# Another order for the later operations of a fused attention and mixer kernel

## The chip, the cores and the metric

The kernel runs on one core of one Trainium2 chip. The metric is device time in microseconds for the whole program, one launch, lower being better. The engines are named as in the profile: PE is TensorE, DVE is VectorE, ACT is ScalarE, POOL is GpSimd and SP is SyncE. Each engine takes its own instructions in the order in which the program wrote them, and waits for others by semaphores.

## What is computed

Eight batches of causal attention in blocks (8 heads, 576 positions, head size 64) are followed by a mixer: two products along the positions ("token") and two along the channels, each pair with a relu between, each with its input added.

```python
def _attn_ref(q, k, v):                      # q, k, v: 8 x 8 x 576 x 64
    scores = scale * np.matmul(q, k.transpose(0, 1, 3, 2))
    mask = block_i >= block_j                # blocks of 64 positions
    scores = np.where(mask, scores, -1000000000.0)
    attn = np.exp(scores - np.max(scores, axis=-1, keepdims=True))
    attn = attn / (np.sum(attn, axis=-1, keepdims=True) + 1e-09)
    return np.matmul(attn, v)

def _moe_ref(x, w_tok1, w_tok2, w_ch1, w_ch2):   # x: 8 x 576 x 512
    h = np.maximum(x.transpose(0, 2, 1) @ w_tok1, 0.0) @ w_tok2
    u = x + h.transpose(0, 2, 1)
    return u + np.maximum(u @ w_ch1, 0.0) @ w_ch2
```

Inputs and output are float32; the matrix products work on bfloat16 copies.

## The kernel before

The kernel first lists all its work as some 1,590 numbered operations, each a closure that emits one or a few instructions, with the operations it depends on. It then emits them in one written order, the text `ORDER`. A word of that text is an operation's number, a letter for its engine (T is PE, A is ACT, D is DVE, P is POOL, S is SP) and, for an operation that opens PSUM banks, a letter for each bank: a to d are the tiles `mm`, e to h the tiles `late`, s and t the two pairs `sc` of the start. So `644Tadgb` is score set 644 on PE in the banks a, d, g and b.

```python
for word in ORDER.split():
    digits = word.rstrip("abcdefghstADPST")
    o, letters = self.ops[int(digits)], word[len(digits):]
    o.engine = self.ENGINE[letters[0]]
    assert all(d.n in done for d in o.deps)
    for letter, (pools, note) in zip(letters[1:], o.take):
        note["pool"], note["slot"], note["home"] = pool_of[letter], self.SLOTS[letter][1], letter
```

The order of the words of one letter is thus the order of that engine's queue; the words decide as well which of two possible engines does an evacuation of PSUM (ACT or DVE), a tail (DVE or POOL) or a late output (SP or ACT). Words of different engines stand in one text because the framework derives the semaphores from the order of emission: an operation emitted later waits for one emitted earlier where they touch the same tile.

The operations of a batch, with the lines under which the profile shows them:

- Loads of q and k (L413, POOL, one DMA each) and their transposition on DVE in halves (L437). For batch 4, 759 loads k and 762 loads q of the first four heads; 760 and 761 transpose k, 763 and 764 transpose q. For batch 3 the second four heads have the transpositions 602, 603 (k) and 605, 606 (q).
- Loads of v (L463, POOL, five DMAs): 607 to 611 for batch 3, 771 to 775 for batch 4, 938 to 942 for batch 5.
- Scores (L562, PE): three sets for each half of the heads, each in four banks, and for each bank an exponential on ACT (L768; L581 in batch 0). For batch 3 the sets are 612, 619, 624 and 644, 651, 656; those of batch 4 begin at 776, of batch 5 at 943, of batch 6 at 1038, of batch 7 at 1136. The first score set of batch 0 is in two parts, 174 and 175, with the exponentials 176 and 177.
- Tails, a small copy and a clearing of part of the exponentials (L590 and L595, POOL or DVE), such as 617 and 618, or 980 and 981.
- Heads: products with v (L612, L665, PE), a reciprocal (L632, L687, DVE) and a scaling (L638, L693, DVE).
- Token products (L803, L807, then L898, L929, PE), relus (L789 on ACT, L791 on DVE) and u additions (L913, DVE), such as 681 and 685, and from batch 2 on a transposition by DMA (L965, L975, SP).
- The first channel product in seven products a group instead of eight (L1099, and L1226 for two batches at once, PE), with sums held back as a copy (`keep`, L395 on ACT or L397 on DVE, such as 547), a copy that seeds two further banks (`seed`, the same lines), joins (L1138 and L1259, DVE, such as 554), relus (L789, L791) and clips (L1151 and L1272 on ACT, L1153 and L1274 on DVE, such as 542). Where a seeded bank was not filled in full before, one opening matmul of 512 columns is put ahead (`cover`).
- The second channel product likewise (L1360, PE), with sums (L1342, DVE) and folds into the output (L1406, DVE), and the outputs (L1451, L1435, SP or ACT).

PE works at the attention of one batch between the channel products of earlier ones: the operations of batch 3's attention stand among those of batch 1's first channel product (526 to 574), batch 4's among batch 2's (690 to 738), batch 5's among batch 3's (857 to 905).

Of the kernel before, what the change touches and what calls it, by code (L numbers as in the profile page):

```python
# [27 lines left out]
class Plan:  # L28
# [73 lines left out]
    23D 25D 21D 31D 7D 174Tst 176A 175T 177A 81Ta 76Tb 195A 197D 196A 33D 198D 60Tc 61Td 201Ts 180Tt 202A 80Ta 35P 182Ts  # L102
# [11 lines left out]
    331D 332D 441A 432D 431D 358T 359A 450Tgceh 427P 429D 322D 323D 428D 369Td 370T 169P 453A 452A 363Tf 364T 335D 454A
    371D 451A 365A 482Tbeac 393D 484A 504Th 336D 470Tgfde 483A 485A 486A 474A 502Tb 472A 503A 471A 445Tacef 447A 505D
    514Th 168P 167P 170D 171D 172D 173D 611P 510Tb 506Tg 598P 599D 511D 394D 448A 446A 515A 508Tc 433P 512Te 513D 509D
    507D 395D 396D 524Ta 473A 397Thd 403Tb 449A 525A 434P 406D 398A 399T 443P 444P 402D 437P 477Tfaec 480A 407T 522Tg
    479A 523A 410D 595P 597D 596D 518Te 519A 411T 412D 436P 435P 455Ta 458Th 461Tg 608P 604P 600D 601P 464Te 475P 476P
    481A 456D 465D 466D 478A 496Tc 462D 516Tf 517A 463D 457D 459D 460D 520Tb 521A 413T 414D 605D 499Te 497D 609P 467Tf
    468D 500D 498D 501D 612Tgbah 616A 613A 615A 614A 469D 415T 545Tgh 526D 493Tc 530Tae 531Tf 527D 494D 533A 487Tb 495D  # L120
# [8 lines left out]
    779A 820Tedgb 585T 824A 821A 823A 577D 690D 781P 782P 694Taf 695Tb 935P 691D 578D 942P 799Te 696D 842Tg 697A 692D
    698Tb 699A 587T 702T 693D 843A 848Tg 586D 800D 801D 700T 849D 589T 588D 703D 701A 822A 590D 808Tegac 930D 932P 931D  # L130
    846Td 793Tb 591T 809A 810A 811A 794D 795D 847D 592D 796Te 797D 798D 812A 938P 813P 814P 815Tgabc 818A 816A 805Td
    806D 928D 941P 704T 705D 724Tbh 819A 802Te 803D 804D 844Tg 807D 845D 706D 725Tc 940P 727A 730T 817A 850Te 851D 726A
    709Tad 854S 937D 712A 828Tc 829D 728Tg 830D 710Te 707T 715T 729A 716A 734T 711A 927D 732T 731D 855S 708D 713Ta
# [10 lines left out]
    1079A 1080A 1081A 594S 1124D 1017Tc 1018D 755T 1123D 1121D 1083A 1015Tb 1034P 756D 1016D 1078A 1037P 1070Tdeca 757S
    1067Tg 1064Th 1068D 1065D 1066D 1073A 1074A 1128P 1058Tf 1059D 1072A 1069D 873D 1125P 1060D 1071A 1130D 1104Tc 1105A
    1133P 1132P 1061Tb 1013Ta 1055Th 1143Tegdf 1014D 1145A 1146A 1056D 1057D 1129D 1062D 1063D 1075P 1076P 1090Tc 1144A
    1091D 1092D 1127D 1102Ta 1103A 1147A 1093Th 1094D 1095D 1136Tgdbe 1137A 1114Tc 1139A 1140A 1126D 1099Ta 1100D 1101D
    1108Tf 1109D 1110Tg 1096Th 1097D 1138A 1141D 1098D 1087Tb 1088D 1115A 1175Teadf 1112Tc 1089D 1011Th 1012D 1019S
    1113D 1179A 1336Tb 1177A 1176A 1178A 1168Tfaeh 1337A 1172A 906D 1171A 1111D 1170A 1106Td 1107D 1116S 910Tbc 907D
    1148Thgea 1149A 1152A 911D 1151A 914Td 1142P 916T 908D 1169A 1180Thaef 1182A 909D 912T 1183A 1173D 1184A 917D 915D  # L150
    1134P 918T 913D 1181A 1174D 1131P 1135P 1162Ta 1163D 1164D 1153Te 1154D 1155D 1191Tf 1192D 1193D 1159Th 1197Tb 1198D
    1160D 1150A 1161D 1117S 1165Tg 1166D 1167D 920T 921D 1199D 1194Ta 1020S 1156Te 1157D 1158D 1185Tf 1334Th 1335A 1186D
    1187D 1188Tg 1189D 1190D 1195D 1196D 922T 1234Thb 923D 856S 1348Te 1237A 1349A 1200D 1249Tcf 1240T 1252A 1241A 919D
    1118S 1201D 1202D 1250Tg 1251D 1235Ta 1236A 1253Td 1254D 1238Te 1279Tah 1255T 1256A 1259T 1239D 1242T 1257T 1203D
    1282A 1243D 1350Tg 1283Tc 1260D 1258D 1285T 1351A 1262T 1263D 1286D 1284A 1204Tde 1280Tg 1244T 1281D 1205Tf 1207A
    1208Ta 1206A 1210T 1360Tg 1209A 1214T 1211A 1361A 924S 1245D 1215D 1264Tdf 1267A 1247T 1212T 1289T 1213D 1290D 1248A
    1287T 1288D 1344Tg 1345D 1217T 1218A 1265Tb 1270T 1219Tac 1266A 1271D 1268Te 1269D 1356Tg 1357D 1222A 1220Tb 1292T
    1293A 1358Td 1359D 1364S 1221D 1223Tg 1274T 1275D 1338Th 1225T 1479D 1224A 1229T 1354Td 1339D 1230D 1355D 1277T
    1278A 1226A 1227T 1228D 1272T 1273D 1232T 1233A 1294D 1295D 1261D 758S 1291A 1342Tb 1343D 1216A 1347S 1352Th 1498Taf
    1298Tcd 1501A 1353D 1362S 1296D 1363S 1297D 1276D 1302Tg 1480D 1481D 1299A 1304T 1305D 1504T 1231A 1483Tbe 1484Th  # L160
    1485A 1300T 1486A 1308T 925S 1246A 1301D 1482D 1303D 1309D 1489T 1314D 1502Tc 1503A 1306T 1307D 1340Th 1341D 1310T
    1505D 1490A 1315D 1487Tg 1488A 1508T 1499Th 1513Tab 1500A 1493T 1311D 1494D 1506T 1514Th 1516A 1517Td 1491T 1519T
    1520A 1509D 1518D 1492D 1515A 1346S 1496T 1523T 1507D 1510D 1521T 1524D 1316D 1511T 1512A 1497D 1414Tag 1312S 1417D
    1318Tch 1319D 1526T 1322Tf 1320T 1317D 1527A 1399Tbe 1402A 1522D 1365D 1415Td 1416A 1324T 1366D 1323D 1325D 1321D
# [1396 lines left out]
```

## Time and profile before

| | |
|---|---|
| three timed runs | 286.66, 287.95, 288.83 us; median 287.95 |
| the profiled execution | 285.7 us, its span in the profile 283.9 us |
| PE, DVE, ACT, POOL busy | 273.1, 247.0, 176.2, 73.7 us |
| granted PE clock | 1.0 throughout |
| moved by DMA | 31.94 MB in 64889 packets |

Times in the profile are microseconds from the start of the span unless marked ns. A row of the timeline gives the start, the length, the engine, the line of the source, the operation and its tiles, a count, and in brackets the idle time of the engine before it with what ended it. A row of the groups gives the count, the busy time, the mean ns of one, and the idle time before them. A row of the stretches gives the length of the stretch and, for each engine, its busy microseconds. Matmuls are pipelined and their shown lengths overlap, so the step between starts is the time that one takes.

### The profile page before, as it was taken

The numbers are of one execution on the slowest core, as the hardware profiler recorded it, in microseconds if no ns is written. First come the engines' busy times: TensorE is split into PE (matmuls) and PEld (weight loads), VectorE is DVE, ScalarE is ACT, GpSimd is POOL, SyncE is SP. The second block draws the span as 40 slices with busy tenths as digits, with TensorE's granted clock in tenths as the row PEclk, the third lists the DMA queues.
The fourth block names the chain that finished last, engine by engine and source line by source line (L and its number), as shares of the span: only waits on it lengthen the run. The fifth ranks groups of instructions, "written<-read, shape, count | busy, mean of one in ns | idle before, by whom it ended". The sixth has DMA issues, their size and how long they took to land.

```text
span 283.9 us, 9275 instructions
## 1 busy us (share of the span) xinstructions
PE 273.1 (96%) x3930; PEld 202.4 (71%) x3956; DVE 247.0 (87%) x525; ACT 176.2 (62%) x322; POOL 73.7 (26%) x125
## 2 busy tenths in 40 slices
PE   6798999999989999999999999999999999999995
PEld 2376574589667788886877668766688976468884
DVE  4578889999789989999999987887899998799994
ACT  3796969955978857799978875256464324634000
POOL 8986626701732054024351030000000000000000
PEclk9999999999999999999999999999999999999999
DMA  7999999992999456949499079012045301400165
GB/s 167 152 156 206 178 213 210 176 118 44 182 190 111 76 77 54 212 97 140 36 161 158 3 64 172 3 74 86 8 46 147 108 0 74 151 0 3 74 180 192
DMA packets 64889, 31.94 MB, mean 113 GB/s; under 512 B 53200, under 2 KB 55888, under 8 KB 64848
## 3 DMA queue, kind: packets, MB, share of 16 engines
q0 software_dynamic: 44896, 17.49, 52.9%
q1 hardware_dynamic: 19232, 12.82, 17.7%
q10 hardware_dynamic: 720, 1.05, 1.0%
q8 instruction: 31, 0.51, 0.7%
q14 instruction: 10, 0.08, 0.1%
HBM read 35.85 MB, written 9.44 MB: 159 GB/s over the span
## 4 chain that ended last, share of the span: by engine, by line
PE 83%; POOL 6%; DMA 5%; ACT 2%; issue 1%; DVE 1%; POOLq 0%
PE mm L1360 16%; PE late L1360 14%; PE late L1226 8%; PE late L1099 7%; PE mm L1226 5%; PE mm L1099 4%; PE late L562 4%; PE mm L562 3%; PE late L612 3%; PE mm L612 3%; DMA w_sb<-in_moe_w_tok_dram 3%; DMA qk_sb<-in_k_dram 3%; POOL vals L463 2%; ACT e_sb L768 2%; PE late L898 2%; PE mm L803 2%
## 5 line engine op out<-in xcount | busy, mean ns | idle before, releaser
L768 ACT ACTIVATE e_sb<-late 128x512 bf16<-128x512 f32 x83 | 48.3, 618 | 11.9 <-PE late L562 6.7
L768 ACT ACTIVATE e_sb<-mm 128x512 bf16<-128x512 f32 x85 | 49.0, 614 | 8.5 <-PE late L562 3.9
L437 DVE STREAM_TRANSPOSE qk_sb<-qk_sb 128x288 int32<-128x288 int32 (+1 forms) x65 | 42.4, 696 | 3.3 <-DMA qk_sb<-in_k_dram 2.2
L463 POOL DMA_DIRECT2D vals<-in_v_dram x45 | 37.3, 850 | 13.0 <-PE late L665 6.1
L1360 PEld LDWEIGHTS <-gT 128*128 128x128 bf16 x336 | 32.0, 98 | 6.0 <-issue 0.4
L1360 PEld LDWEIGHTS <-sums 128*128 128x128 bf16 x324 | 31.2, 98 | 5.3 <-issue 1.5
L562 PEld LDWEIGHTS <-qk_sb 32*64 32x64 bf16 (+1 forms) x1152 | 19.5, 103 | 17.1 <-issue 12.4
L562 PE MATMUL late<-qk_sb 32*64 32x64 bf16 (+7 forms) x494 | 27.9, 279 | 0.9 <-DVE gT L1138 0.7
L562 PE MATMUL mm<-qk_sb 32*64 32x64 bf16 (+7 forms) x514 | 27.6, 280 | 0.3 <-DVE qk_sb L437 0.2
L612 PEld LDWEIGHTS <-e_sb 128*128 128x128 bf16 x640 | 23.7, 97 | 4.1 <-issue 1.4
L1099 PEld LDWEIGHTS <-ws_sb 128*128 128x128 bf16 x192 | 18.2, 98 | 3.4 <-issue 0.9
L395 ACT COPY mm<-late 128x512 f32<-128x512 f32 x24 | 14.1, 592 | 10.3 <-PE late L1226 4.1
L590 POOL COPY vals<-e_sb 128x256 bf16<-128x256 bf16 x10 | 5.1, 506 | 51.6 <-ACT e_sb L768 51.6
L1226 PEld LDWEIGHTS <-ws_sb 128*128 128x128 bf16 x120 | 11.7, 98 | 8.1 <-issue 0.4
L789 ACT ACTIVATE gT<-late 128x512 bf16<-128x512 f32 x20 | 12.2, 619 | 8.0 <-PE late L1226 4.7
L612 PE MATMUL mm<-vals,e_sb 128*128 128x65 bf16 x370 | 15.8, 193 | 0.5 <-DMA vals<-in_v_dram 0.4
L638 DVE TENSOR_TENSOR x_sb<-mm,rinv 128x256 bf16<-128x256 f32 x37 | 15.4, 420 | 0.9
L1099 PEld LDWEIGHTS <-wc_sb 128*128 128x128 bf16 x144 | 15.1, 114 | 1.4 <-issue 0.4
L1226 PEld LDWEIGHTS <-wc_sb 128*128 128x128 bf16 x90 | 10.1, 113 | 5.7
L1360 PE MATMUL mm<-wd_sb,sums 128*128 128x256 bf16 x114 | 13.9, 273 | 0.0
L1226 PE MATMUL late<-e_sb,ws_sb 128*128 128x512 bf16 (+1 forms) x54 | 13.5, 356 | 0.0
L581 ACT ACTIVATE e_sb<-sc 128x1024 bf16<-128x1024 f32 (+2 forms) x14 | 11.6, 908 | 2.2 <-PE sc L562 2.2
(205 smaller groups left out, 653.3 us busy)
## 6 DMA issues: line engine op xcount, KB each, us to landing
out_dram<-o_sb SPq DMA_DIRECT2D x18, 256.0 KB, 2.4
qk_sb<-in_q_dram POOLq DMA_DIRECT2D x14, 288.0 KB, 6.4
qk_sb<-in_k_dram POOLq DMA_DIRECT2D x14, 288.0 KB, 6.3
vals<-in_v_dram POOLq DMA_DIRECT2D x28, 128.0 KB, 6.5
out_dram<-o_sb SPq DMA_DIRECT2D x7, 512.0 KB, 3.2
wc_sb<-in_moe_w_ch_dram POOLq DMA_DIRECT2D x8, 192.0 KB, 6.9
wc_sb<-in_moe_w_ch_dram POOLq DMA_DIRECT2D x3, 512.0 KB, 11.7
vals<-in_v_dram POOLq DMA_DIRECT2D x15, 64.0 KB, 5.3
```

The costliest lines, as they stand in the source:

```text
L395: nc.scalar.copy(dst, src)
L437: nc.vector.transpose(dst[:, 0:S, :] .rearrange("p s e -> p (s e)") .bitcast(I32) .rearrange("p (a k) -> p k a", k=NB)[:, k0:k1], raw2.bit ...
L463: nc.gpsimd.dma_start(out=t[128 - p : 128, J, hs, 0:64], in_=src)
L562: nc.tensor.matmul(out=home(n)[lo : lo + rows, c : c + w], lhsT=bar[r, 0] if j is None else kT[i][r, 64 * j : 64 * j + rows, par], rhs=bar ...
L581: nc.scalar.activation(dst, sc[SC.index(note["pool"])][:, :, cols], EXP, scale=scale)
L612: nc.tensor.matmul(out=u[:, I, 0:65], lhsT=e[:, h, c : c + 128], rhs=vt[:, J, head, 0:65], start=(J == 0), stop=(J == I),)
L638: nc.vector.tensor_tensor(out=xt[:, 0:4, 64 * head : 64 * head + 64], in0=u[:, :, 0:64], in1=ri[:, 0:4].to_broadcast([128, 4, 64]), op=MULT,)
L768: nc.scalar.activation(dst, bank_of(x), EXP, scale=scale)
L789: nc.scalar.activation(dst, src, RELU)
L1099: nc.tensor.matmul(out=bank_of(bank)[:, 256 * o_ : 256 * o_ + 256], lhsT=x(o_, m), rhs=y[:, :, m, :], start=opens, stop=m == 1, skip_group ...
L1226: nc.tensor.matmul(out=bank_of(bank)[:, 128 * c : 128 * (c + step)], lhsT=x(m), rhs=y[:, c : c + step, m, :], start=opens, stop=m == 1, sk ...
L1360: nc.tensor.matmul(out=bank_of(bank)[:, 256 * i : 256 * i + 256], lhsT=x[:, kk, 128 * i : 128 * i + 128], rhs=y[:, kk], start=first and i ...
```

## The change

Only the text `ORDER` changes. Word by word, the numbers are the same; what changes is their order, the bank letters and, for 73 operations, the engine. First, 175 moves ahead of 176:

```diff
-    23D 25D 21D 31D 7D 174Tst 176A 175T 177A 81Ta 76Tb 195A 197D 196A 33D 198D 60Tc 61Td 201Ts 180Tt 202A 80Ta 35P 182Ts
+    23D 25D 21D 31D 7D 174Tst 175T 176A 177A 81Ta 76Tb 195A 197D 196A 33D 198D 60Tc 61Td 201Ts 180Tt 202A 80Ta 35P 182Ts
```

From there to batch 3's attention only bank letters differ. From then on the order is another one. The part around the scores of batch 3:

```diff
-    490Tc 532A 418D 488D 491D 489D 492D 548A 536T 537A 534Td 535A 551T 602D 552A 624Tfbca 628A 625A 626A 528D 538T 539D
-    549Tg 550D 529D 540T 541D 627A 678Ta 679A 762P 617P 618P 619Tfdbc 622A 543T 544A 607P 620A 623A 546Ta 606D 759P 764D
-    761D 547A 676Tb 773P 621A 603D 760D 677A 553T 560Tce 774P 554D 555T 775P 563A 561Tf 763D 644Tadgb 562A 648A 566T
-    556D 646A 645A 684Tf 557D 567D 420S 685D 564Tb 647A 610P 558T 559A 565D 680Td 651Tcafg 655A 542D 652A 654A 653A 768P
...
+    490Tf 532A 418D 488D 491D 489D 492D 548A 536T 537A 534Te 535A 551T 602D 762P 617P 618P 607P 759P 773P 420S 419S 610P
+    528D 624Thgfb 552A 538T 606D 628A 540T 529D 627A 539D 678Ta 626A 603D 625A 549Tb 679A 619Tfegh 541D 550A 546Ta 622A
+    760D 553T 623A 763D 543T 620A 547D 676Tg 621A 761D 544A 644Thfae 542D 926P 677A 554D 555T 647A 764D 560Tbc 648A 556D
+    561Tg 929P 563A 680Ta 557D 765P 562A 684Te 681D 645A 566T 558T 685D 646A 564Ta 567A 649D 559D 651Tghfe 650P 565A
...
```

The part around the second half of batch 5's scores, where 1008 and 1010 change their engine:

```diff
-    892Te 991A 893D 593S 895Ta 1027P 890A 896A 1030P 1007Tb 1008A 740D 955Tdgef 959A 901T 741D 958A 956A 1009Tb 1022D
-    957A 989A 899T 960Tf 902D 904T 1010A 975Tedgc 972Tb 905A 900D 1026D 961D 962D 1035P 966Ta 967D 978A 976A 977A 743Thf
...
+    887D 1034P 990A 895Tf 988A 875D 889T 991A 1007Th 740D 989A 896A 890D 955Tdegb 741D 892Tc 959A 899T 1026D 956A 901T 893D
+    958A 1009Tb 957A 1008D 902D 975Tdgce 1010D 972Th 978A 904T 900D 979A 960Tb 1025D 969Tc 905A 743Tef 961D 976A 973D
...
```

And the end, with the last outputs:

```diff
-    1584T 1585D 1589A 1562T 1563D 1568S 1566T 1567D 1569A 1586T 1587D 1590A
+    1577D 1585D 1566T 1589A 1583D 1556T 1588A 1567D 1562T 1569S 1557D 1586T 1563D 1568S 1587D 1590S
```

On PE one instruction pair is added: product 1249 (L1226) gets one opening matmul.

More of the change, by code (lines that the diff above doesn't have):

```diff
@@ L114 @@
[L114 to L118, printed above, removed]
@@ L129 @@
[L129 to L133, printed above, removed]
@@ L144 @@
[L144 to L163, printed above, removed]
@@ new lines @@
+    1282A 1350Tb 1256A 1281A 1234Tcg 1351A 1344Td 1237A 1283Tb 1345D 1285T 1284A 1240T 1286A 1338Te 1241A 1250Td 1339D
+    1253Th 1251A 1287T 1202D 1254A 1348Tc 1288D 1203D 1259T 1349A 1257T 1238Tb 1258D 1289T 1239A 1235Te 1290D 1342Td
+    1236A 1244T 1291D 1343D 1356Tc 1242T 1245D 1219Tdh 1243D 1360Te 1260D 1220Tb 1361A 1357D 1262T 1222A 1292T 1364S
+    1263D 1221A 1340Te 1247T 1293D 1223Tb 1341D 1358Tc 1224A 1246D 1204Taf 1359D 1248A 1205Te 1225T 1207D 1206A 1264Tcg
+    1226A 1229T 1479D 1267A 1265Te 1230D 1208Td 1266A 1227T 1480D 1209D 1270T 1268Te 1271A 1214T 1269D 1212T 1354Tc
@@ new lines @@
+    1215D 1274T 1228D 1232T 1275D 1217T 1272T 1481D 1218A 1210T 1482D 1233A 1273D 1277T 1211A 1483Tbf 1278D 1347S 1484Th
+    1352Te 1294D 1485A 1298Tag 1295D 1363S 1302Th 1296D 1299A 1486A 1353D 1304T 1355D 1297D 1362S 1300T 1231D 1305D
+    1487Tc 1301D 1346S 1308T 1303D 1498Tae 1309D 1306T 1501A 1213D 1488A 1276D 1310T 1307D 1504T 1311D 1491T 1505A 1489T
+    1261D 1313S 1493T 1312S 1490A 1513Tad 925S 1502Tb 1516A 1499Th 1503D 1514Tg 1500A 1519T 1492D 1508T 1494D 1520A
+    1506T 1509D 1517Ta 1515A 1496T 1216D 1518A 1314D 1511T 1414Tch 1512A 1507D 1521T 1523T 1522D 1510A 1318Tbg 1524D
@@ new lines @@
+    1417A 1365D 1526T 1366D 1420T 1415Te 1315D 1421A 1322Ta 1416A 1527D 1319A 1497D 1418Tc 1316D 1320T 1419A 1367D
+    1429Tde 1321D 1324T 1432A 1317D 1323D 1424T 1435T 1425D 1422T 1436A 1433Tb 1368D 1326T 1423D 1434A 1325D 1430Tf
+    1327D 1439T 1431A 1427T 1332S 1399Tad 1428A 1328T 1402D 1440D 1437T 1405T 1438D 1442T 1406A 1384Tcf 1441D 1443A
+    1329D 1385Th 1387A 1403Ta 1400Tb 1386A 1330T 1404A 1401A 1409T 1331D 1407T 1390T 1333S 1408D 1369Tbe 1391A 1444Tgh
+    1410D 1372A 1388Ta 1412T 1389A 1375T 1413D 1447A 1373Tc 1394T 1525D 1374A 1376D 1370Td 1450T 1395D 1371A 1448Tb
@@ new lines @@
+    1426D 1392T 1449A 1445Td 1393D 1451A 1379T 1446A 1454T 1495D 1380D 1452T 1396A 1377T 1455D 1382T 1397T 1457T 1398A
+    1532Tag 1458D 1383A 1459D 1463Tdf 1460D 1467Te 1461D 1464A 1462D 1469T 1533D 1528D 1465T 1468D 1536Th 1466D 1453D
+    1471T 1529D 1456A 1470D 1538T 1530D 1378D 1473T 1472D 1381A 1411D 1477S 1534T 1531D 1474D 1574Tbd 1570D 1554Tce
+    1535D 1575A 1571D 1475T 1555A 1550D 1537D 1576T 1539D 1540T 1476D 1551D 1478S 1580T 1552D 1542T 1541D 1547S 1578Ta
+    1546S 1543D 1560T 1572D 1544T 1573D 1581D 1553D 1558Tf 1561D 1545D 1564T 1579D 1548S 1549A 1559D 1584T 1565D 1582T
```

67 lines of the change are left out of this document (39 added, 28 removed).

## The prediction

> **What bounds the kernel now.** I read the page first, then the busy time by stretches, then the waits of TensorE, and then the order of time around the one long wait.
>
> ```profile
> span 283.9 us, 9275 instructions
> PE 273.1 (96%) x3930; PEld 202.4 (71%) x3956; DVE 247.0 (87%) x525; ACT 176.2 (62%) x322; POOL 73.7 (26%) x125
> PEclk9999999999999999999999999999999999999999
> ```
>
> TensorE is busy 96% of the span, at the full granted clock in all slices. VectorE stands at 87%, so it is the second bound. Both must be seen by stretch:
>
> ```profile
> core 0: us, PE busy (x) PEld busy (x) DVE busy (x) ACT busy (x) POOL busy (x), PEclk, DMA share, GB/s
> 72.00:88.00 16.00, 14.94 (x225) 10.21 (x226) 13.23 (x26) 13.90 (x28) 8.24 (x13) 1.00 1.40 178
> 106.00:120.00 14.00, 13.89 (x280) 11.87 (x280) 13.82 (x31) 10.14 (x20) 3.30 (x5) 1.00 1.00 123
> 120.00:132.00 12.00, 12.00 (x170) 10.08 (x167) 11.26 (x26) 11.35 (x22) 4.62 (x8) 1.00 0.68 116
> 132.00:146.00 14.00, 13.95 (x309) 10.51 (x309) 12.92 (x30) 12.70 (x26) 4.79 (x8) 1.00 0.80 100
> 146.00:163.00 17.00, 16.79 (x375) 12.31 (x377) 16.40 (x44) 14.26 (x29) 3.03 (x5) 1.00 0.75 99
> ...
> 184.00:210.00 26.00, 25.84 (x179) 17.78 (x180) 21.97 (x36) 16.13 (x28) 0.00 (x0) 1.00 0.14 46
> 210.00:240.00 30.00, 29.95 (x249) 24.79 (x249) 26.96 (x44) 11.18 (x19) 0.00 (x0) 1.00 0.38 89
> 240.00:281.00 41.00, 40.70 (x313) 30.62 (x310) 37.29 (x66) 11.25 (x18) 0.00 (x0) 1.00 0.28 90
> ```
>
> From 184 us on TensorE idles 0.5 us in 97: nothing is to be gained there by any order. Only the stretch 72 to 88 us shows a real hole, 1.06 us. From 106 to 163 us TensorE is full, and VectorE nearly so: 54.40 of 57 us. An order that asks more of VectorE there finds little room.
>
> ```profile
> PE sc L562 <- ACT e_sb L581: 0.9, 2, 0.6
> PE late L562 <- DVE gT L1138: 0.7, 1, 0.7
> ```
>
> These are the waits that the change can touch directly: the second part of the first score set (0.6), and one score set of batch 3 (0.7).
>
> **The first score set.**
>
> ```profile
> 8.46 0.49 ACT L581 ACTIVATE e_sb<-sc 128x384 bf16<-128x384 f32 x1 [1.17 <-PE sc L562]
> 9.00 0.34 PE L562 MATMUL sc<-qk_sb 32*64 32x320 bf16 x4 [0.63 <-ACT e_sb L581]
> 9.54 0.70 ACT L581 ACTIVATE e_sb<-sc 128x640 bf16<-128x640 f32 x1 [0.59 <-PE sc L562]
> ```
>
> Now the second part (175) waits 0.63 us for the exponential of the first (176). Set right behind, 175 starts near 8.4 and takes the 0.45 us that lie between 9.00 and the exponential at 9.54, less the 0.1 us of the handover. But in the changed program the one wait on TensorE stands at 176 and 177 has none, so 176 now starts behind both parts, near 8.95, ends near 9.45, and 177 follows at once, against 9.54 now. ScalarE's chain of exponentials behind it gains 0 to 0.1 us; TensorE's 0.6 us only let it wait for the next bank. I take 0.
>
> **Batch 3, around score set 644.**
>
> ```profile
> 71.73 0.55 POOL L413 DMA_DIRECT2D qk_sb<-in_k_dram  x1
> 71.73 7.24 DMA qk_sb<-in_k_dram
> 76.02 1.25 DVE L437 STREAM_TRANSPOSE qk_sb<-qk_sb 128x288 int32<-128x288 int32 x2
> 78.99 1.79 DVE L437 STREAM_TRANSPOSE qk_sb<-qk_sb 128x288 int32<-128x288 int32 x3 [1.73 <-DMA qk_sb<-in_k_dram]
> 80.63 0.68 DVE L1138 TENSOR_TENSOR gT<-late,half 128x512 bf16<-128x512 f32 x1
> 79.53 0.60 PE L1099 MATMUL late<-th_sb,ws_sb 128*128 128x256 bf16 x4
> 81.36 0.30 PE L562 MATMUL late<-qk_sb 32*64 32x320 bf16 x1 [0.73 <-DVE gT L1138]
> 85.44 0.44 PE mm L1099 x4
> 82.47 0.43 DVE L1153 TENSOR_SCALAR gT<-gT 128x1024 bf16<-128x1024 bf16 x1
> ```
>
> Load 759 (k of batch 4) is issued at 71.73 and lands at 78.97. VectorE stands at its transposition 761 from 77.26 on and waits 1.73 us; behind 761 are queued 603 (which 644 needs), 760 and the join 554, which frees a bank that 644 takes. So 644 opens in full at 81.36, while its turn on TensorE was at 79.53 + 0.44 = 79.97: a loss of 1.4 us.
>
> In the new order 603 stands ahead of the transpositions of batch 4, which would cure this. But 760 is the first of them now, and VectorE reaches it even earlier, near 76. GpSimd's queue up to 759 and 773 is the same as now, so I let 759 land at 78.97 again. Behind 760 are queued 763 and the copy 547, which ScalarE does now. 644 takes bank a, held by product 546, and 547 is what frees it. Two transpositions at the step of 0.55 us (three take 1.79 from the first start to the last end, 0.69 of it the last) and a copy of 0.68 end at 80.77. So 644 opens near 80.8, 0.55 us earlier than now. Yet products 560, 555 and 561 stand ahead of it now and behind it then: 3 x 0.44 = 1.31 us of work not yet done. Net some 0.75 us later. Next, 560 takes the bank of join 554, and VectorE still has 761, the clip 542 and 554 to do: 0.55 + 0.45 + 0.6 from 80.77, so 82.4; 560's turn, behind 644 (0.6 us) and 555, is at 81.85: 0.55 us more. Some 0.1 us for the two u additions 681 and 685, each a place later on VectorE. Sum +1.4 us. Bounds: if the load lands after the median of its kind and 554 is in time, 0.75 - 0.94 = -0.2; if the whole wait goes, -1.4; with another two such steps, +2.2. I take +1.4, since the load's place in its queue is unchanged.
>
> ```profile
> qk_sb<-in_k_dram POOLq DMA_DIRECT2D x14, 288.0 KB, 6.3
> ```
>
> **From batch 4's attention on, where VectorE is full.** The change moves work between the engines.
>
> ```profile
> L789 ACT ACTIVATE aT<-mm 128x512 bf16<-128x512 f32 x9 | 5.7, 636 | 0.4 <-PE mm L807 0.3
> L791 DVE TENSOR_SCALAR gT<-mm 128x512 bf16<-128x512 f32 x10 | 6.8, 680 | 0.3
> L397 DVE COPY mm<-late 128x512 f32<-128x512 f32 x10 | 6.8, 692 | 0.3 <-PE late L1226 0.2
> L590 DVE COPY vals<-e_sb 128x256 bf16<-128x256 bf16 x4 | 0.8, 208 | 0.0
> L595 DVE MEMSET e_sb<- 64x128 uint32 x3 | 0.5, 165 | 0.3
> ```
>
> Around the scores of batch 5, both token relus of batch 4 (1008, 1010), and copy 864 and relus 875 and 890 of the channel products of batch 3, go from ScalarE to VectorE, and the tail 980, 981 from GpSimd: 4 x 0.68 + 0.69 + 0.21 + 0.17 = 3.79 us. Copy 879, relu 883, clip 873 and the tail 1043, 1044 leave it: 0.69 + 0.68 + 0.43 + 0.21 + 0.17 = 2.18. VectorE gets 1.6 us more in the stretch from 120 to 146 us, where it idles 0.74 + 1.08 = 1.82. If every idle piece can be used, this costs nothing; if none can, 1.6. Head products wait there for the reciprocal and the scaling of the heads before, which stand behind the added relus in one queue. I take the middle, +0.8. Before that, around the scores of batch 4, VectorE loses relus 708, 723, 731 (2.04 us) and gets copy 727 and clips 721, 736 (1.55): 0.5 us less, but TensorE idles only 0.11 us in 106 to 120, so the gain is 0.
>
> Around the scores of batch 7, token relu 1335 (0.68) goes to VectorE and part of the tails leaves it; the stretch from 146 to 163 us has 0.60 us idle. Between 0 and 0.7; I take +0.3, because the token product 1336 of the new order stands directly in front of the score set 1168, behind the same heads.
>
> **The queues of GpSimd and SyncE.** 771, 775 and 774 (v of batch 4) are issued only behind 932, 941 and the tail copy 781, later than now; but their first reader, head 793, is moved back too. 940, 942 and 938 (v of batch 5) likewise, with heads 972 and 960 as readers.
>
> ```profile
> vals<-in_v_dram POOLq DMA_DIRECT2D x28, 128.0 KB, 6.5
> ```
>
> Counting TensorE's work between issue and reader by the durations above, some 7.6 to 10.4 us stand against 6.5 to landing: hidden by 1 to 4 us, so 0; with landings 2 us later, as in a burst, +1 each, which I keep for the upper end. On SyncE the token transpositions 688, 689, 854, 855 stay ahead of their readers by more than now, and the outputs moved past them (594 ahead of 854) wait for folds that are done. 0.
>
> **The last 100 us.** Net nine copies, relus and clips go from VectorE to ScalarE, which has 11 of 30 us busy there. TensorE has nothing to win, so 0. Product 1249 gets one opening matmul more, 512 columns, by
>
> ```profile
> 236.58 1.29 PE late L1226 x6
> ```
>
> 0.2 us. The last two outputs go from ScalarE's to SyncE's queue; each is issued when its fold is done, 0 to 0.3 us, taken as 0.
>
> **Sum.** 0 + 1.4 + 0.8 + 0.3 + 0 + 0.2 = +2.7 us. The profiled execution took 285.7 us (span 283.9 and 1.8 around it); it would take 288.4. The median of the runs shown, 287.95, stands 2.25 above the profiled one, so I forecast 290.6 us, 0.9% more.
>
> **Rivals.** First, that the wait at 644 goes for good. For it: 603 stands ahead now, and the two v loads 774 and 775 no longer follow 759 on the queues, so 759 may land earlier, one us by the median row and perhaps two; then 547 and 554 are in time and 1.4 us are won, with nothing lost later if VectorE's idle pieces can be used: 287.95 - 1.4 + 0.2 = 286.8. It decides in full when 759 lands before 76.9, 1.78 us ahead of the new turn of 644 at 79.97 - 1.31 = 78.66. To be faster by over 1%, 2.9 us, it must win another 1.5 us of the small holes of the later stretches (0.11 + 0 + 0.05 + 0.21 us in 106 to 163); against it stands how little they hold. Chance 0.20, of which 0.07 below that bound.
>
> Second, VectorE sets the pace from 120 to 163 us: its added 1.6 and 0.7 us count in full, 771 to 774 and 938 to 942 land late by 1 us each, and batch 3 takes its upper 2.2: 287.95 + 2.2 + 1.6 + 0.7 + 2 + 0.2 = 294.6; half of it, 292.5, is likelier. Against it: 1.82 us of idle time lie there. Chance 0.16.
>
> Third, the orders are worth the same: the load at 78.97 sets both at batch 3, the rest fits: 288.2. Chance 0.08.
>
> Fourth, the wait at 644 grows until the clock drops. Now the clock never does, in spite of the hole. The first matmuls of the kernel, before the clock is up, show the price:
>
> ```profile
> L367 PE MATMUL mm<-wd_sb 128*128 128x512 bf16 x11 | 4.3, 573 | 1.2 <-DVE wd_sb L340 1.2
> L374 PE MATMUL mm<-wd_sb 128*128 128x512 bf16 x10 | 2.8, 381 | 0.2 <-issue 0.2
> ```
>
> 573 against 381 ns over eleven is 2.1 us. TensorE would stand at 644 from 78.7 to 80.8, 2.1 us; a load 1.4 us later makes the gap 3.5 us and gives, if the clock drops, 290.6 + 1.4 + 2.1 = 294.1. [...] Chance 0.04.
>
> **How the numbers follow.** The forecast case has 0.52 and spans 288.9 to 292.7 by its bounds. 1% is about what a measurement of this kernel can tell from no change; that bound above is 290.8, so half of the case, 0.26, counts as the same. Faster 0.07. Same 0.13 + 0.08 + 0.26 = 0.47. Slower 0.26 + 0.16 + 0.04 = 0.46. The range goes from 286.2, just under the first rival, to 294.6, the second.
>
> **What would show it.** Right: VectorE waits 2 to 3 us for the k load before a transposition near 76 us, TensorE's longest wait in batch 3 is for a copy on VectorE (L397) and comes 1.3 us of products earlier; VectorE is over 95% busy from 120 to 146 us; TensorE stays full from 190 us on. Wrong: no TensorE wait near 80 us, a load that lands before 77, holes of over 1 us anywhere behind 163 us, or head products (L612) that wait for v.

## The result, and the profile after

Over 20 runs of each the kernel before takes 286.95 us (285.52 to 289.11) and the changed kernel 288.69 us (286.70 to 291.77): ratio 1.0065, 95% interval 1.004 to 1.009, some 1.9 us more. The medians are those of all runs, while a ratio leaves out the few slow ones, over 1.5% above the fastest of their kernel. The profiled execution of the changed kernel takes 288.03 us with a span of 286.1, that of the kernel before 285.7 with 283.9.

First the page of the changed kernel, then its busy time by stretches:

```profile
span 286.1 us, 9279 instructions
PE 273.0 (95%) x3934; PEld 201.9 (71%) x3957; DVE 241.0 (84%) x518; ACT 177.3 (62%) x329; POOL 73.7 (26%) x125
PEclk9999999999999999999999999999999999999999
```

```profile
72.00:88.00 16.00, 13.98 (x227) 10.51 (x227) 12.03 (x28) 13.57 (x28) 6.10 (x10) 1.00 0.96 143
120.00:132.00 12.00, 12.00 (x188) 10.28 (x186) 11.76 (x29) 10.16 (x20) 7.21 (x11) 1.00 1.02 128
132.00:146.00 14.00, 13.95 (x254) 10.51 (x253) 13.51 (x35) 11.83 (x24) 2.85 (x5) 1.00 0.89 123
146.00:163.00 17.00, 16.84 (x433) 12.61 (x436) 15.84 (x37) 14.11 (x29) 4.68 (x8) 1.00 0.83 99
```

TensorE's hole in 72 to 88 us grows from 1.06 to 2.02 us. From 120 to 146 us VectorE is busy for 25.27 of 26 us, as forecast (24.18 before), yet TensorE idles there for no more than 0.05 us, as before.

The waits, and the order of time around score set 644:

```profile
PE mm L562 <- DVE half L397: 1.9, 1, 1.9
DVE qk_sb L437 <- DMA qk_sb<-in_k_dram: 5.4, 2, 3.4
```

```profile
79.73 0.33 PE L562 MATMUL late<-qk_sb 32*64 32x320 bf16 x2
80.09 1.26 DVE L437 STREAM_TRANSPOSE qk_sb<-qk_sb 128x288 int32<-128x288 int32 x2 [3.39 <-DMA qk_sb<-in_k_dram]
81.19 0.68 DVE L397 COPY half<-mm 128x512 f32<-128x512 f32 x1
81.93 0.30 PE L562 MATMUL mm<-qk_sb 32*64 32x320 bf16 x1 [1.86 <-DVE half L397]
```

VectorE stands at the transposition 760 for 3.39 us, until the k load has landed; behind it the first two transpositions and the copy 547 end near 81.9, and only then does score set 644 have its bank. It is one hole of 1.86 us where there were two before, 0.2 and 0.7 us.

To compare executions I counted TensorE's products, each with the median step of its kind, and read from each trace when the same amount of work was done. "Work" is this count in microseconds: work 60 is reached when products worth 60 us are done. The table gives how far an execution lags behind the profiled one of the kernel before; the last column is the time from TensorE's end to the end of the span. e1 to e11 are the experiments below.

```
at work (us)            60     72     76     84     272    end of PE to end of span
before                   0      0      0      0      0      3.22
changed               +1.00  +0.98  +1.79  +1.76  +1.26    4.04
e2 (changed, ACT)     +1.26  +1.24  +2.42  +2.39  +2.02    3.41
e8 (changed, relus)   -0.37  -0.39  +0.85  +0.82  +0.31    4.05
e3                    +0.03  +0.01  -1.35  -0.54  -1.01    4.09
e5                    +0.60  +0.58  -0.78  +0.27  -0.23    3.59
e6                    -0.05  -0.06  -1.43  -0.35  -0.84    3.53
e11                   -0.01  -0.03  +1.49  +2.16  +1.66    3.88
e1 (before, edit 1)   +1.23  +1.23  +1.67  +1.66  +1.67    3.21
e4                    +0.02  +0.02  -1.25  -0.49  -0.47    3.19
e7 (before, SP)       +1.37  +1.37  +1.61  +1.60  +1.63    3.23
```

Three things are seen in it. The start (to work 60) differs from execution to execution by 1.6 us where the order is the same up to there (e8 and e2), and by 1.4 in the order of before (e6 and e7). Batch 3 (72 to 84) costs 0.8 to 1.2 us in the three executions with the changed order around 644 and the full clock. And what follows, to work 272, is not dearer in the new order but cheaper, by 0.4 to 0.5 us in all seven rows that have it; the rows with the old order stay within 0.03.

### The profile page after: what moved, and what is told of

Its sections match the earlier page's. It is cut to its first block, busy times and chain, and to the rows that moved or that the text cites. A ratio compares the mean times of both kernels' runs of the same rounds, so it can differ in the third digit from the quotient of the medians.

```text
span 286.1 us, 9279 instructions
## 1 busy us (share of the span) xinstructions
PE 273.0 (95%) x3934; PEld 201.9 (71%) x3957; DVE 241.0 (84%) x518; ACT 177.3 (62%) x329; POOL 73.7 (26%) x125
## 4 chain that ended last, share of the span: by engine, by line
PE 74%; DMA 10%; POOL 6%; DVE 5%; issue 3%; ACT 0%; POOLq 0%; DVEq 0%
PE late L1360 19%; PE mm L1360 9%; PE late L1226 8%; PE mm L1099 7%; DMA qk_sb<-in_k_dram 5%; PE mm L1226 5%; PE late L1099 5%; PE mm L562 3%; PE mm L612 3%; DMA qk_sb<-in_q_dram 3%; PE late L562 3%; PE mm L803 2%; DMA vals<-in_v_dram 2%; PE late L898 2%; PE late L612 2%
## 5 line engine op out<-in xcount | busy, mean ns | idle before, releaser
L768 ACT ACTIVATE e_sb<-late 128x512 bf16<-128x512 f32 x92 | 51.5, 606 | 15.9 <-PE late L562 6.6
L768 ACT ACTIVATE e_sb<-mm 128x512 bf16<-128x512 f32 x76 | 43.2, 606 | 10.5 <-PE late L562 5.7
L562 PE MATMUL mm<-qk_sb 32*64 32x448 bf16 (+7 forms) x472 | 24.8, 278 | 2.5 <-DVE half L397 1.9
L612 PEld LDWEIGHTS <-e_sb 128*128 128x128 bf16 x640 | 22.7, 97 | 4.5 <-issue 2.8
L395 ACT COPY mm<-late 128x512 f32<-128x512 f32 (+1 forms) x24 | 13.5, 571 | 18.2 <-PE late L1226 8.7
L1360 PE MATMUL late<-wd_sb,sums 128*128 128x256 bf16 x156 | 19.0, 273 | 0.0
L612 PE MATMUL mm<-vals,e_sb 128*128 128x65 bf16 x410 | 17.2, 193 | 1.0 <-DMA vals<-in_v_dram 1.0
L638 DVE TENSOR_TENSOR x_sb<-mm,rinv 128x256 bf16<-128x256 f32 x41 | 17.2, 421 | 1.1
L1226 PEld LDWEIGHTS <-ws_sb 128*128 128x128 bf16 x120 | 11.7, 98 | 8.6 <-issue 0.2
L1360 PE MATMUL late<-wd_sb,gT 128*128 128x256 bf16 x144 | 17.7, 273 | 0.0
L789 ACT ACTIVATE gT<-mm 128x512 bf16<-128x512 f32 x25 | 15.0, 611 | 3.8 <-PE mm L1099 2.8
L1099 PEld LDWEIGHTS <-wc_sb 128*128 128x128 bf16 x144 | 15.1, 114 | 1.5 <-issue 0.4
L1406 DVE TENSOR_TENSOR o_sb<-late,u_sb 128x512 f32<-128x512 f32 x18 | 12.3, 683 | 3.6 <-PE late L1360 3.6
L1226 PE MATMUL late<-e_sb,ws_sb 128*128 128x512 bf16 (+1 forms) x70 | 15.1, 330 | 0.1
```

The costliest lines, as they stand in the source:

```text
L395: nc.scalar.copy(dst, src)
L562: nc.tensor.matmul(out=home(n)[lo : lo + rows, c : c + w], lhsT=bar[r, 0] if j is None else kT[i][r, 64 * j : 64 * j + rows, par], rhs=bar ...
L612: nc.tensor.matmul(out=u[:, I, 0:65], lhsT=e[:, h, c : c + 128], rhs=vt[:, J, head, 0:65], start=(J == 0), stop=(J == I),)
L638: nc.vector.tensor_tensor(out=xt[:, 0:4, 64 * head : 64 * head + 64], in0=u[:, :, 0:64], in1=ri[:, 0:4].to_broadcast([128, 4, 64]), op=MULT,)
L768: nc.scalar.activation(dst, bank_of(x), EXP, scale=scale)
L789: nc.scalar.activation(dst, src, RELU)
```

## The experiments

**The first edit alone (e1).**

```diff
- 174Tst 176A 175T 177A
+ 174Tst 175T 176A 177A
```

> The kernel before with the first edit alone: 175 stands ahead of 176. Theory: the edit is worth nothing, ratio to before 0.998 to 1.002; TensorE loses its wait of 0.63 us at the second part, the first exponential starts 0.5 us later, the second near the same time as now. Rival A: the edit delays ScalarE's chain and with it the start, which explains that the changed kernel's profile was 1.0 us behind already at batch 3: ratio 1.003 or more, token products of batch 0 later by 0.5 to 1 us. Rival B: the edit gains the 0.5 us of its wait: ratio 0.998 or less.

Measured: 287.75 us, ratio 1.0022 (0.9981 to 1.0062). No answer by itself: the profiled execution lags by 1.23 us from the start on, but e7 lags as much without the edit. e5 and e6 say more below.

**The last large outputs on ScalarE again (e2)**, in the changed kernel:

```diff
- 1569S 1557D 1586T 1563D 1568S 1587D 1590S
+ 1569A 1557D 1586T 1563D 1568S 1587D 1590A
```

> The changed kernel with the outputs 1569 and 1590 back on ScalarE's queue. Between the end of TensorE's work and the end of the span lie 3.2 us before and 4.0 us after. Theory: SyncE's queue as the last issuer costs this 0.8 us, of it 0.5 in its final drain; with ScalarE as the issuer the tail is 3.2 to 3.5 us again and the ratio to before falls from 1.0065 to 1.004. Rival: the 0.8 us comes from the outputs that stand closer together at the end, whoever issues them: tail 3.8 to 4.0, ratio 1.006.

Measured: 288.43 us, ratio 1.0053 (1.0023 to 1.0082). From TensorE's end to the end of the span it takes 3.41 us instead of 4.04. The ratio moves in the same direction, by less than the intervals can tell apart.

**The transpositions of batch 4 later, in the changed kernel (e3).**

```diff
- 760D 553T 623A 763D 543T 620A 547D 676Tg 621A 761D 544A 644Thfae 542D 926P 677A 554D 555T
+ 553T 623A 543T 620A 547D 676Tg 621A 544A 644Thfae 542D 677A 554D 760D 763D 761D 926P 555T
```

> The changed kernel with VectorE's transpositions 760, 763 and 761 (q and k of batch 4) moved behind copy 547, clip 542 and join 554, and the load 926 behind them. Theory: the wait of score set 644 for copy 547 (1.86 us, and 0.3 more at its first matmuls) is only the queue behind the k load; it goes, join 554 is in time, and 1.7 to 2.2 us are won: ratio to before 0.999 to 1.001. Rival: VectorE is the bound in this stretch, so the transpositions only make the next joins late and less than 0.7 us are won: ratio 1.004 or more.

Measured: 286.11 us, ratio 0.9992 (0.9955 to 1.0029). The order of time, VectorE first, then the one wait that TensorE has left there:

```profile
76.98 0.69 DVE L397 COPY half<-mm 128x512 f32<-128x512 f32 x1 [1.24 <-PE mm L1099]
79.27 2.34 DVE L437 STREAM_TRANSPOSE qk_sb<-qk_sb 128x288 int32<-128x288 int32 x4 [0.66 <-DMA qk_sb<-in_k_dram]
```

```profile
83.96 0.36 PE L562 MATMUL late<-qk_sb 32*64 32x448 bf16 x1 [0.43 <-DVE u_sb L913]
```

The copy 547 comes at 76.98 instead of 81.19 (in an execution that started 1.0 us earlier), VectorE waits 0.66 us for the load instead of 3.39, and the hole at 644 is gone. Against the changed kernel this wins 2.17 us by work 76, of which 1.33 are left at 84: the u additions (L913) now stand behind four transpositions in a row, and the next score set waits 0.43 us for one.

**The same cure in the kernel before (e4).**

```diff
- 606D 759P 764D 761D 547A 676Tb 773P 621A 603D 760D 677A 553T 560Tce 774P 554D 555T
+ 606D 603D 759P 764D 547A 676Tb 773P 621A 677A 553T 560Tce 774P 554D 761D 760D 555T
```

> The kernel before with 603 ahead of 764 and with 761 and 760 behind join 554 on VectorE: the same cure for its own wait at 644 (TensorE idle 0.17 and 0.73 us, its turn missed by 1.4 us). Theory: 1.2 to 1.5 us won, ratio 0.995 to 0.996. Rival: given back at the next joins, less than 0.5 us won, ratio 0.998 or more.

Measured: 285.83 us, ratio 0.9989 (0.9952 to 1.0025). The lag is -1.25 us at work 76, as hoped, but only -0.49 at 84: VectorE's queue keeps the sum of the work, and 0.8 us come back at the u additions. Theory and rival part there, and it is the rival that holds: less than 0.5 us is won.

**Both cures together (e5), and without the first edit (e6).** e5 is e3 with 1569 and 1590 on ScalarE as in e2; e6 is e5 with 176 ahead of 175 again. Some names in the texts on record, here and for e9 to e11, are wrong: 760, 761, 763 and 764 are all transpositions of batch 4's k and q, none of them a value addition or of batch 3, and 926 loads the k of batch 5.

> The changed kernel with both cures at once: batch 3's second transposition (760), its two value additions (763, 761) and batch 4's k load (926) behind VectorE's 554, and the two last large outputs (1569, 1590) issued by ScalarE. Theory (the change costs 0.6 to 1.3 us at score set 644 and 0.6 to 0.8 us behind PE's end, and these are separate sums): PE ends near 280.0 us in an execution that starts like the one of before, the stretch from PE's end to the end of the span is 3.2 to 3.5 us, the span 283.2 to 283.6, and the ratio to the kernel before 0.994 to 0.998. Rival 1 (the 0.8 us behind PE's end is the queue of output transfers, not the engine that issues the last one): the stretch stays at 3.9 to 4.1 and the ratio at 0.999. Rival 2 (the first edit costs 1 us at the start, as the profiled execution of the changed kernel has it): ratio 1.000 to 1.002.

> The kernel of the run before this one, with the first edit undone (175 stands behind 176 again, as in the kernel before). Theory (the first edit costs nothing; the start differs from execution to execution): the median lies within 0.5 us of that run, on either side. Rival (setting 175 early costs the 1.0 us that the changed kernel lags by at 60 to 72 us): the median is 0.8 to 1.2 us below that run, and the lag of PE behind the kernel before at 60 us of work is 0 to 0.1 us here and 1.0 there in most executions.

Measured: e5 285.65 us, ratio 0.9950 (0.9926 to 0.9973); e6 285.15 us, ratio 0.9953 (0.9927 to 0.9978). The version that the experiments point to is thus faster than both kernels, by 0.5% than the one before. The first edit is worth nothing that can be measured: the two ratios differ by 0.0003, the medians by 0.5 us, where the intervals reach some 0.7 us to each side.

**SyncE issues the last outputs of the kernel before (e7).**

```diff
- 1568S 1566T 1567D 1569A 1586T 1587D 1590A
+ 1568S 1566T 1567D 1569S 1586T 1587D 1590S
```

> The kernel before with its two last large outputs (1569, 1590) issued by SyncE, as in the changed kernel; nothing else. Theory (SyncE issuing the last output costs, since its closing drain comes 0.5 us behind the last landing and the transfer itself is 0.3 us longer): from PE's end to the end of the span 3.9 to 4.1 us instead of 3.2, ratio 1.002 to 1.003. Rival (the closer spacing of all the last outputs in the changed kernel makes its 4.04 us): the stretch stays at 3.2 to 3.4 and the ratio at 1.000.

Measured: 287.05 us, ratio 1.0008 (0.9984 to 1.0033), and 3.23 us at the end. My theory fails: in the order of before SyncE as the issuer costs nothing. Only in the new order, where outputs follow each other more closely (the last seven are issued within 4.9 us in the changed kernel, within 6.8 in the kernel before), do the five kernels with SyncE (changed, e3, e8, e10, e11) take 3.88 to 4.09 us and the three with ScalarE 3.41 to 3.59.

**Two relus back on ScalarE (e8)**, in the changed kernel. 1008 and 1010 are relus of a token product; the text on record names them wrongly.

```diff
- 957A 1008D 902D 975Tdgce 1010D
+ 957A 1008A 902D 975Tdgce 1010A
```

> The changed kernel with the two exponentials' masking operations 1008 and 1010 back on ScalarE, as in the kernel before; nothing else. By the term of the prediction (VectorE full from 120 to 146 us costs PE 0.8 us, of which these two operations are a half) the time falls by 0.4 to 0.8 us against the changed kernel and the ratio comes to 1.003 to 1.005. Theory from the traces (PE lost nothing in 120 to 146 us although VectorE was busy for 25.27 of 26 us): PE's lag behind the kernel before does not change by over 0.2 us between work 120 and 163, and the ratio stays within 0.002 of the changed kernel's 1.0065. Rival on the other side (ScalarE then delays the exponentials that score sets wait for): PE waits for ScalarE between 118 and 130 us and the ratio rises to 1.008 or more.

Measured: 289.44 us over 8 runs, ratio 1.0079 (1.0049 to 1.0109).

```profile
132.00:146.00 14.00, 13.95 (x304) 10.44 (x305) 12.69 (x34) 12.46 (x24) 2.66 (x4) 1.00 0.90 119
```

VectorE has 0.82 us less to do there than in the changed kernel, and TensorE is busy for the same 13.95 us. From work 84 to 272 the lag falls by 0.51 us in e8 and by 0.50 in the changed kernel: the fuller VectorE took nothing from TensorE. The ratio lies close to the 1.008 of the rival on the other side, but that rival's wait is missing: in the profiled execution no wait of TensorE is listed between 118 and 163 us. The wait at 644 stays (2.30 us here), and the time does not fall.

**The granted clock.** Every run gives its mean granted clock, and here the kernels differ. A stretch of 3.41 us at half clock, the shortest that the traces show ahead of the end, takes 0.006 off the mean of 286 us (e7 and e11, with one in their profiles, show 0.994), so by this estimate an execution at 0.9965 or more had none in full. At 0.9965 or more were 56 of 83 executions of the kernel before (22 of 35, 22 of 31 and 12 of 17 beside three sets of experiments), and 5 and 6 of 12 of e1 and e7, which have its order there, but 4 of 20 of the changed kernel, 1 of 12 of e2 and 1 of 8 of e8, which have the hole (1.86, 2.24 and 2.30 us in their profiles); of e3, e4, e5 and e6, which have none, 7, 7, 9 and 9 of 12. So without a long hole, too, over a third of the executions (56 of 155) is below. In the changed kernel the four have a median of 287.59 us and the other sixteen 288.98. The last three kernels test whether the hole does that. The first puts such a hole into the kernel before (e9), the second makes it longer (e10), the third shorter (e11):

```diff
- 759P 764D 761D 547A 676Tb 773P 621A 603D 760D 677A 553T 560Tce 774P 554D 555T 775P 563A 561Tf 763D 644Tadgb
+ 759P 761D 547A 676Tb 773P 621A 603D 760D 764D 763D 677A 553T 560Tce 774P 554D 555T 775P 563A 561Tf 644Tadgb
```

> The kernel before with VectorE's transposition 764 and value addition 763 moved behind 760, so that both stand between the k load and the join 554 that score set 644 waits for; nothing else. TensorE's two holes there (0.2 and 0.7 us) become 0.2 and about 2.0 us, as long as the single hole of the changed kernel (1.9 us). Theory (a hole of about 2 us in TensorE does not only cost itself: in most executions a stretch at a lower granted clock follows, which is why the changed kernel has a mean granted clock of 0.9965 or more in 4 of 20 executions and the kernel before in 22 of 35): at most 4 of 12 executions have 0.9965 or more, and the ratio is 1.005 to 1.009 (1.4 us of hole less 0.4 given back, and 0.6 to 1.0 us of clock). Rival (the clock does not depend on this hole; the changed kernel's lower clock has its cause elsewhere): 6 to 9 of 12 executions at 0.9965 or more, and a ratio of 1.002 to 1.005.

```diff
- 763D 543T 620A 547D 676Tg 621A 761D 544A 644Thfae 542D 926P 677A 554D 555T 647A 764D
+ 763D 761D 764D 543T 620A 547D 676Tg 621A 544A 644Thfae 542D 926P 677A 554D 555T 647A
```

> The changed kernel with the value addition 761 and the transposition 764 ahead of the copy 547 on VectorE, so that TensorE's hole ahead of the second half of score set 644 grows from 1.9 to about 3.3 us; nothing else. Theory (the hole lowers the granted clock): no more than 1 of 12 executions has a mean granted clock of 0.9965 or more, and the profile shows a granted clock under 0.8 in a stretch of 2 to 4 us that begins within 8 us behind the hole; against the changed kernel 1.0 to 1.4 us for the hole and up to 0.8 for the clock, ratio 1.010 to 1.014. Rival (clock independent of the hole): the granted clock is 1.00 in 76 to 96 us, the share of executions stays at a fifth, ratio 1.009 to 1.011.

```diff
- 760D 553T 623A 763D 543T 620A 547D 676Tg 621A 761D 544A 644Thfae 542D 926P 677A 554D 555T
+ 760D 553T 623A 543T 620A 547D 676Tg 621A 761D 544A 644Thfae 542D 926P 677A 554D 763D 555T
```

> The changed kernel with the value addition 763 moved behind the join 554, so that the copy 547 follows the transposition 760 directly and TensorE's hole shrinks from 1.9 to about 1.2 us (a second of up to 0.5 us may stay ahead of products that wait for 554's successors); nothing else. Theory: with a hole between those of the kernel before (0.7 and 0.2 us) and of the changed one, 5 to 9 of 12 executions have a mean granted clock of 0.9965 or more, and the ratio falls from 1.0065 to 1.001 to 1.004. Rival: the share stays at a fifth, and the ratio falls by the 0.4 to 0.7 us of the hole alone, to 1.004 to 1.005.

Measured: e9 289.28 us over 6 runs, ratio 1.0104 (1.0072 to 1.0136), none of the 6 at 0.9965 or more; e10 290.50 us over 6 runs, ratio 1.0152 (1.0118 to 1.0186), none of 6; e11 287.39 us, ratio 1.0038 (1.0007 to 1.0069), 7 of 12. Both larger holes cost a little more than the theory had said. In e9 two operations moved on VectorE make TensorE's wait 1.8 us, and the kernel before is then no faster than the changed one. For e11 the ratio lies in both ranges; the share alone speaks for the theory. What the shares leave open is where the half clock lies. The profiled execution of e9 had it from 9 to 29 us, far ahead of the hole, and the full clock behind the hole; so its low mean is not the hole's, and for the other five no trace shows the place.

```profile
PE late L562 <- DVE gT L1138: 1.8, 1, 1.8
```

The traces show where the clock goes. Ahead of the end of the program the half clock lasted 3.41 us in e7 and e11, 3.41 and 6.83 us in e10 and 20.48 us in e9, each a whole multiple of 3.41. Within an execution the changes of the clock lie a whole multiple of that apart, too: in e10 the half clock begins at 20.25 and again at 81.69 us, 18 x 3.413 later; in the kernel before and in the changed one the record of the full clock begins at 4.82 and at 6.46 us and lasts 279.89 us, 82 x 3.413. A window is here a stretch of 3.41 us on the grid that these changes give; its phase differs from execution to execution. Cut along that grid, e10 (hole 2.7 us), e11 (in this execution 1.7 us, not the 1.2 expected; e8, which starts alike, has 2.3) and the changed kernel's profiled execution (1.9 us); the columns are TensorE's busy time, its weight loads, VectorE, ScalarE, GpSimd, then the granted clock:

```profile
78.28:81.69 3.41, 1.46 (x9) 0.60 (x8) 2.08 (x4) 1.92 (x4) 0.00 (x0) 1.00 1.45 165
81.69:85.10 3.41, 2.59 (x50) 1.98 (x50) 2.21 (x5) 1.08 (x2) 1.73 (x3) 0.50 0.65 98
85.10:88.52 3.42, 3.20 (x13) 1.82 (x13) 1.82 (x4) 2.15 (x4) 0.00 (x0) 0.50 0.89 168
88.52:91.93 3.41, 3.41 (x71) 2.65 (x70) 2.15 (x8) 2.80 (x6) 1.72 (x3) 1.00 0.40 61
```

```profile
78.23:81.64 3.41, 1.70 (x51) 1.05 (x50) 2.17 (x5) 1.31 (x4) 0.03 (x1) 1.00 1.15 130
81.64:85.05 3.41, 3.19 (x14) 1.97 (x14) 3.00 (x6) 2.73 (x6) 1.59 (x3) 0.50 0.63 92
85.05:88.46 3.41, 3.41 (x72) 2.82 (x71) 2.52 (x7) 2.67 (x6) 1.72 (x3) 1.00 0.99 146
```

```profile
78.14:81.55 3.41, 1.87 (x13) 1.01 (x12) 1.46 (x3) 2.33 (x5) 0.00 (x0) 1.00 1.49 171
81.55:84.97 3.42, 2.99 (x60) 2.43 (x61) 3.38 (x8) 2.24 (x5) 1.29 (x3) 1.00 0.32 31
```

The window with TensorE busy for 1.46 us of 3.41 and the one with 1.70 were followed by a window at half clock; the one with 1.87 us was not. The kernel before has 2.46 us in the window of its two holes:

```profile
79.91:83.32 3.41, 2.46 (x57) 1.72 (x56) 3.23 (x7) 2.18 (x6) 1.43 (x2) 1.00 1.72 185
```

The other three profiled executions with a long hole say the same: e2 (hole 2.24 us), e8 (2.30) and e9 (1.81), all at the full clock behind it:

```profile
78.40:81.82 3.42, 1.87 (x13) 1.00 (x12) 1.09 (x2) 2.33 (x5) 0.00 (x0) 1.00 1.51 180
```

```profile
76.57:79.98 3.41, 2.07 (x15) 1.20 (x14) 0.82 (x2) 2.52 (x6) 0.00 (x0) 1.00 1.49 183
79.98:83.40 3.42, 2.36 (x56) 2.01 (x57) 3.42 (x7) 1.61 (x4) 0.66 (x2) 1.00 0.30 21
```

```profile
84.09:87.50 3.41, 2.37 (x21) 1.72 (x20) 2.25 (x5) 2.86 (x6) 0.70 (x2) 1.00 2.05 200
87.50:90.91 3.41, 2.16 (x54) 1.86 (x55) 2.68 (x6) 1.39 (x3) 0.73 (x1) 1.00 1.32 190
```

By these rows the length of the hole alone does not decide it: behind 1.7 us in e11 came a slow window, behind 2.3 us in e8 none. In e8 and e9 the grid cut the hole (2.07 and 2.36, 2.37 and 2.16 us busy in its two windows), and in the changed kernel and e2 a little over half of the window was busy (1.87 us); none of the four had a slow window behind. That the phase of the grid decides it in each execution fits the shares above but is not shown: there are only these six profiled executions with a long hole, two of them with a slow window. e11, with one window at half clock, loses 2.19 us between work 72 and 84; the changed kernel, with a longer hole and the full clock, loses 0.78.

## Why the prediction was right, and where its sum was not

The forecast of 290.6 us (+2.7) had the sign and the place; 1.0 of the 1.9 us by which it lies above the 288.69 comes from its base, the median of three runs, 287.95, where twenty give 286.95. The rest is a sum whose terms err on both sides:

- First edit, taken as 0: right, by e5 against e6, as far as their intervals tell.
- Batch 3, taken as +1.4: right in mechanism, too large by a step. The load landed at 80.00, 7.27 us behind its issue (7.24 before), 760, 763 and 547 stood behind it in that order, and score set 644 opened 1.86 us late. Lag +0.8 to +1.2 us. (The order of before itself shows +0.2 and +0.4 there in e7 and e1, so that the lower figure is the better one.) That is the 0.75 us net that the prediction had for 644; the 0.55 us that product 560 was to wait for join 554 did not come, since the wait of 1.86 us is the only one of TensorE in the list from 72 to 92 us. The cure in e3 removes the wait and the loss.
- VectorE full from 120 to 163 us, taken as +0.8 and +0.3, and +0.2 for the cover product: the step that failed. VectorE did become that full, but TensorE's busy time stayed at 12.00 and 13.95 us and was 16.84 against 16.79, and from work 84 on the new order wins 0.4 to 0.5 us. Idle time that VectorE lost cost TensorE nothing here, and e8, which gives VectorE 0.82 us of it back, wins nothing by it. Where the 0.4 to 0.5 us come from was not tested.
- The last outputs, "0 to 0.3, taken as 0": mis-sized. The end takes 4.04 us instead of 3.22; 0.45 to 0.65 us of it go with SyncE's outputs (e2, e5, e6), 0.2 to 0.4 with the closer order.
- The clock, a rival with a chance of 0.04 and a price of 2.1 us, added up for a gap of 3.5 us (a load 1.4 us later): by the shares a lower clock is what mostly comes, with a hole of about 2 us and at less than that price. No run shows that it takes such a gap: a slow window came behind a hole of 1.7 us in e11 and of 2.7 us in e10, and none behind 2.3 us in e8. The price itself stands in the trace of before: ahead of 4.82 us, where the record of the full clock begins, the median product of L367 takes 634 ns, behind it 380. The share of executions at the full clock falls from 56 of 83 to 6 of 40 (changed, e2, e8), 0.52, and in the changed kernel an execution below it takes 288.98 - 287.59 = 1.4 us longer: 0.7 us on average, if that were the price in both kernels. In the kernel before the medians of the two kinds differ by 1.7 to 2.6 us, and with that the difference is some 0.4 us.

Together, 0.8 to 1.2 (batch 3) - 0.5 (later) + 0.1 (behind work 272: at TensorE's end the lag is 1.4 us, not 1.26) + 0.8 (end) + 0.4 to 0.7 (clock) = 1.6 to 2.3 us, against 1.9 (1.1 to 2.6) measured. So it is in part luck that the sum came within 1 us: 1.65 us of terms that did not come (0.55 at 560, 1.1 for VectorE) stand against the 0.8 us of the end and the 0.4 to 0.7 us of the clock that it did not have. The first rival, that the wait at 644 goes for good, did not happen, since the load took 7.27 us to land as against 7.24; e3 shows what it would have brought. The second, VectorE as the bound, is excluded by TensorE's rows from 120 to 163 us and by e8. The third, no difference, lies outside the interval.

Two figures of the prediction are not what they are called. 292.5, "half" of the second rival, halves only the terms of VectorE and of the loads; half of all its 6.7 us is 291.3. And the bounds given for the terms put the lower end of the forecast case at 287.95 (-0.2 + 0 + 0 + 0.2), not at 288.9.

Of what the prediction said one would see, the 3.39 us wait for the k load, the copy of L397 as the longest wait and VectorE above 95% (25.27 of 26 us) all stand in the rows. Of the signs against it one is there in words: a head product (L612) waits 1.02 us for v, but it starts at 22.20 us, far ahead of the changed part, and the kernel before has such a wait of 0.39 us. The load landed behind 77 us, no hole of over 1 us stands behind 163 us, and from 190 to 282 us TensorE is busy for 91.89 of 92 us.

Left open: what the new order wins behind batch 3, and why SyncE's closing steps come late in the new order only. In the changed kernel the last output lands at 284.67 us, 1.46 before the end of the span; in the kernel before, e2, e6 and e7 it is 0.9 to 1.0. Also, e5 and e6 gain 1.4 us in time but, beside the start, only about 0.5 in the profiled lag and end; the profiled execution of the kernel before has one of the better starts, and that was not separated further.

## What to carry to other kernels

On an engine that takes its queue in order, put what waits for a load behind what the bound engine waits for: one early transposition held back a copy by some 3 us, and moving four words cured it. But add up what else stands behind the moved work, as 0.8 us of it came back a few operations later, in both orders. And a hole in TensorE of some 2 us may have to be priced with more than its length: in the kernels with one hole of about 2 us most executions had a lower clock (34 of 40 of the changed kernel, e2 and e8), with the two short holes of the order before fewer did (40 of 107).

## What the runs showed of the hardware

- In batch 3 the granted clock dropped to half for one or two whole windows of 3.41 us behind a window in which TensorE was busy for half of the time or less (1.46 us in e10, 1.70 in e11). A slow window behind a hole of 1.7 us I had not expected. In the thirteen profiled executions no window between 72 and 92 us that was busy for 1.87 us or more at full clock had a slow one behind it. The bound is rough: only two executions lie below it, the ends of matmuls are modelled, e10 stayed at half clock for a second window although TensorE was busy for 2.59 us of the first, and at the start of the kernel a window busy for 1.60 us of 3.41 had no slow one behind it in the kernel before, while in e10 one busy for 2.14 us had. What else counts is open:

```profile
4.82:8.23 3.41, 1.60 (x30) 0.74 (x29) 2.47 (x6) 1.01 (x3) 3.41 (x7) 1.00 1.05 161
```

```profile
16.84:20.25 3.41, 2.14 (x62) 1.72 (x63) 1.62 (x9) 2.26 (x3) 1.97 (x4) 1.00 1.47 159
20.25:23.67 3.42, 3.39 (x45) 2.36 (x50) 2.25 (x7) 1.57 (x3) 2.82 (x6) 0.50 1.22 179
```

- The start takes up to 1.6 us longer in one execution than in another with the same order up to there (e2 against e8); in e7 a window at half clock goes with its lag of 1.4 us, and e9, with six such windows, is not counted here:

```profile
9.13:12.54 3.41, 3.08 (x31) 0.78 (x35) 1.55 (x5) 1.68 (x3) 3.32 (x6) 0.50 1.71 136
```
